# Falling decays by a backward scan, and the weight conversion in a written order

## The chip, the cores and the metric

The kernel runs on one core of one Trainium2 chip. The metric is device time in microseconds (us) of one execution; smaller is better. PE is the matrix engine (TensorE), DVE the vector engine, ACT the scalar engine, POOL GpSimd, SP the engine that issues most transfers. Every engine takes its instructions strictly in the order in which the program lists them, and engines wait for each other by semaphores.

## The reference

Shapes: q, k, v and f_logit are 4 batches x 8 heads x 768 tokens x 48; then x is 3072 tokens x 384, w_in 384 x 2048, w_out 2048 x 384. The two weights reach the kernel as 64-bit floats.

```python
f = 1.0 / (1.0 + np.exp(-f_logit))
for t in range(S):
    state = f[:, :, t, :, None] * state + np.einsum('bhd,bhe->bhde', k[:, :, t], v[:, :, t])
    y[:, :, t] = np.einsum('bhd,bhde->bhe', q[:, :, t], state)
...
h = x @ w_in                      # x: y with the heads next to each other
g = np.where(h > 0.0, h, np.exp(np.minimum(h, 0.0)) - 1.0)
return g @ w_out
```

## The kernel before

Tokens go in 12 units of U = 256 (three to a batch). Of each unit the kernel makes the attention, and then the MLP on PE: `up(P)` multiplies x with 256 columns of w_in, ACT makes Relu and Exp of it (`exped`), DVE joins them to the ELU (`elu`), and `down(P)` multiplies with 256 rows of w_out. P counts these pieces, eight to a unit. The units 0 and 1 use plain products; later ones use a scheme with fewer multiplications.

**Decays.** 1/f = 1 + exp(-f_logit) is made on ACT (`gates`). `grow` multiplies it up along the tokens with a scan on DVE; `fall` takes the reciprocal of all 256 values, which are the falling decays. k is multiplied with the first and q with the second (`scale`, on POOL). Heads go in pairs p = 0, 1, 2 of a layout of 64 rows each; the fourth pair (index NKT) is spread over the others' gaps: its decays are gathered by PE (`place`, psR), copied back by ACT, and its k and q are scaled then. `transposed`, `advance` (psU), `scores` (psS), `mask`, `step` (the states), `outputs` and `carried` (psY) finish the attention. Unit 0 goes through this first, with `first_outputs` in place of the last two; its x tile is what up(0) waits for.

**Weights.** The 64-bit words come in 16 parts of 768 KB, in the order in which they are needed: wi0, wi1, wi2, wo0, wi3, wo1, wi4, wo2, wi5, wo3, wi6, wo4, wi7, wo5, wo6, wo7 (parts 0 to 15; wi is a piece of w_in, wo of w_out). A part goes through `split` (two DVE operations, L628 and L632), `lower` (ACT, L638) and `merge` (DVE, L646), each of which needs the one before. `merge(n)` also issues `fetch(n + 7)`, since there are seven raw buffers; `split` has two buffers for its bits, so split(n) needs merge(n - 2).

**Order.** The program lists the work by hand. While units 0 and 1 go through the MLP, steps T = 0 to 31 alternate: an even T holds up(T/2), an odd T holds down(T//2 - 2). What stands at a step ahead of it comes from a table that `at_step` fills: attention of unit 1 at the steps in A1 (`both(1)` is advance, scores, mask and states), the fetch of unit 2 (`load(2)`) at step 8. Ahead of each even step stands the elu of the piece before. merge(n) stands two or three steps ahead of the step that needs the part, and split and lower two steps ahead of their merge, behind that step's own products. A transfer takes one of eight completion semaphores in turn, SP's and ACT's from one round, and its issue waits until the last transfer on that semaphore has landed.

Of the kernel before, what the change touches and what calls it, by code (L numbers as in the profile page):

```python
# [8 lines left out]
FP32 = mybir.dt.float32  # L9
# [4 lines left out]
ALU = mybir.AluOpType  # L14
# [342 lines left out]
def fast(ctx: ExitStack, tc: tile.TileContext, q, k, v, f_logit, w_in, w_out, out, flag, outer):  # L357
# [97 lines left out]
    NB = 2  # L455

    qkf = [
        {n: cst.tile([128, HP, 2, U] if n == "f" else [128, HP, U], FP32, name=f"{n}{i}") for n in "fqk"}
        for i in range(NB)
    ]  # L460
    src = {"q": q, "k": k, "f": f_logit}
# [4 lines left out]
    def load(u, names="fkqv"):  # L466
        b, s0 = u // UPB, (u % UPB) * U
        for n in names.replace("v", ""):
            to = qkf[u % NB][n][MAIN]
            frm = src[n][b, :, :, s0 : s0 + U].rearrange("(p r) d s -> (r d) p s", r=2)  # L470
            if n == "f":
                to, frm = to[:, 0:NKT, 0], frm[:, 0:NKT]
            nc.sync.dma_start(out=to, in_=frm)
            for r in range(2 if n == "f" or n == "k" and u > 1 else 0):
                gap = qkf[u % NB][n][GAP[r] : GAP[r] + PAD, 0:NKT]
                nc.sync.dma_start(
                    out=gap[:, :, 0] if n == "f" else gap,
                    in_=src[n][b, 2 * NKT + r, :, s0 : s0 + U].rearrange("(i j) s -> i j s", i=PAD),
                )
        if "v" in names:  # L480
            nc.sync.dma_start(
                out=vs[u % NB][:, :, PAD : PAD + DM], in_=v[b, s0 : s0 + U].rearrange("(c t) n -> t c n", t=W)
            )
# [186 lines left out]
    def gates(u, pieces=(NKT,), bias=1):  # L670

        p = 0
        for n in pieces:
            a = qkf[u % NB]["f"][:, p : p + n, 0]
            nc.scalar.activation(a, a, AF.Exp, scale=-1.0)
            if bias:
                nc.scalar.activation(a, a, AF.Copy, bias=1.0)
            p += n

    def scale(u, *todo):  # L680

        t = qkf[u % NB]
        for n, p, e in todo:
            e.tensor_tensor(out=t[n][:, p], in0=t[n][:, p], in1=t["f"][:, p, "kq".index(n)], op=ALU.mult)  # L684

    def grow(u, p):

        g = qkf[u % NB]["f"][:, p, 0]
        nc.vector.tensor_tensor_scan(out=g, data0=g, data1=g, initial=1.0, op0=ALU.mult, op1=ALU.max)  # L689

    def fall(u, p):

        f = qkf[u % NB]["f"]
        nc.vector.reciprocal(f[:, p, 1], f[:, p, 0])  # L694
# [9 lines left out]

    def place(u, which, bank, pairs=range(NKT)):

        f = qkf[u]["f"]
        if 0 in pairs:
            placed[u, which] = ps.tile([128, U], FP32, tag=bank, name=f"psR{u}_{which}")
        to = placed[u, which]  # L710
        for p in pairs:
            nc.tensor.matmul(to[:], lhsT=rows[:, p], rhs=f[:, p, which], start=p == 0, stop=p == NKT - 1)  # L712
        if NKT - 1 in pairs:
            nc.scalar.copy(f[:, NKT, which], to[:])  # L714

    def decays(u, p):
        grow(u, p)
        fall(u, p)
        scale(u, ("k", p, nc.gpsimd))
        if p:  # L720
            scale(u, ("q", p - 1, nc.gpsimd))
        if p == NKT - 1:
            move(u, slice(0, 2), nc.sync if u > 1 else nc.scalar)

    def watch(u):
        nc.vector.scalar_tensor_tensor(
            out=fine[:], in0=qkf[u % NB]["f"][:, 0:NKT, 0, U - 1 :], scalar=LIMIT, in1=fine[:],
            op0=ALU.is_le, op1=ALU.mult,
        )

# [26 lines left out]
    def step(u, c):  # L757

        if u % UPB == UPB - 1 and c == NC - 1:
            return  # L760
        new = pus[u][c % 2][:, c // 2]
        box = boxes[(u * NC + c) % len(boxes)]
        s = box[:].rearrange("n (p d) -> n p d", d=64)[:, 0:HP, PAD:]
        if u % UPB or c:
            old = sts[u, c][:].rearrange("n (p d) -> n p d", d=64)[:, 0:HP, PAD:]
            nc.vector.tensor_tensor(out=s, in0=new, in1=old, op=ALU.add)
        else:
            nc.scalar.copy(s, new)
        if c == NC - 1:
            end = qkf[u % NB]["f"][:, :, 1, U - 1 :].broadcast_to([128, HP, D])  # L770
            nc.vector.tensor_tensor(out=s, in0=s, in1=end, op=ALU.mult)
        sts[(u, c + 1) if c < NC - 1 else (u + 1, 0)] = box

# [89 lines left out]
    def first_outputs(part):  # L863
# [31 lines left out]
                            )  # L895
        if part == 0:
            for b in range(2):
                nc.scalar.copy(between[:, :, 0:NKT], first_y[b][:, :, :, 0])
# [7 lines left out]
    plan, later, hooks = {}, {}, []  # L906

    def at_step(step, *todo):
        plan.setdefault(step, []).extend(todo)

    def both(u):

        advance(u)
        mask(u, scores(u, ("m3", "m0")))
        while hooks:
            hooks.pop(0)()
        if u == 1:
# [296 lines left out]
    for c in range(NC - 1):
# [64 lines left out]
    def all_down(P):  # L1279
        for _ in down(P):  # L1280
            pass

    for T in range(PLAIN_UP * NFT):
        P = T // 2
        if T % 2 == 0 and P and P != NP:
            elu(P - 1)
        for f in plan.pop(T, ()):
            f()
        if T % 2 == 0:
            up(P)  # L1290
        elif P >= LAG:
            all_down(P - LAG)
        for n in later.pop(T, ()):
            split(n)
            if n not in (A1[2], A1[2] + 1, NFT - 1):
                lower(n)
# [30 lines left out]
    for s in range(5 * total // 2):  # L1327
# [84 lines left out]
```

## Time and profile before

| | us |
|---|---|
| median of 3 runs (545.68 to 546.71) | 545.69 |
| the profiled execution | 544.88 |
| its span | 542.5 |
| PE busy in it | 531.3 |
| DVE busy | 407.0 |
| ACT busy | 317.0 |
| POOL busy | 339.2 |

In the rows of the timeline the first number is the start in us from the span's start, the second the length of the group, then engine, line, operation, output and input with their sizes, the count, and in brackets the idle time of the engine just ahead of it and what ended it. A matmul of 32-bit floats shows as two records, so an `up` of six matmuls reads x12.

### The profile page before, as it was taken

To read this page: it belongs to the slowest core of one execution; us is meant where nothing else is said; L and a number is where in the kernel's file an instruction comes from. 1 tells how busy PE (TensorE), PEld (TensorE's weight loads), DVE (VectorE), ACT (ScalarE), POOL (GpSimd) and SP (SyncE) were. 2 spreads that over 40 slices of the span, in tenths; PEclk is the share of its full clock that TensorE was granted. 3 is DMA by queue.
4 is the path that set the end of the run, shared out by engine and by line. 5 is a ranking of instruction groups with operands and counts; after the bars stand their busy time and mean duration, and the time that the engine had idled before them with its cause. 6 is when DMAs were issued, how large, how long until landed. Compare 5 with 4: busy or idle time off the path is not lost.

```text
span 542.5 us, 15672 instructions
## 1 busy us (share of the span) xinstructions
PE 531.3 (98%) x6308; PEld 496.4 (91%) x6308; DVE 407.0 (75%) x717; ACT 317.0 (58%) x649; POOL 339.2 (63%) x560
## 2 busy tenths in 40 slices
PE   7999999999999999999999999999999999999996
PEld 3677778899999999999999999999999999999995
DVE  8898979866978887687787687687777876645563
ACT  4578774146564576566567467566665565574441
POOL 8320237688898398298298298388478467464452
PEclk9989999999999999999999999999999999999999
DMA  8999961023152271161271261262252212210001
GB/s 210 252 257 250 266 188 45 3 66 90 38 127 73 62 196 37 57 201 31 62 202 32 60 189 47 60 159 76 62 145 89 62 35 77 60 39 1 30 1 37
DMA packets 39347, 53.91 MB, mean 99 GB/s; under 512 B 4288, under 2 KB 29088, under 8 KB 39264
## 3 DMA queue, kind: packets, MB, share of 16 engines
q1 hardware_dynamic: 38848, 52.51, 36.4%
q8 instruction: 52, 0.85, 0.7%
q10 hardware_dynamic: 416, 0.30, 0.2%
q14 instruction: 31, 0.25, 0.2%
HBM read 45.02 MB, written 4.72 MB: 92 GB/s over the span
## 4 chain that ended last, share of the span: by engine, by line
PE 91%; DMA 5%; DVE 2%; SPq 0%; issue 0%; POOL 0%; ACT 0%; DVEq 0%; ACTq 0%; POOLq 0%
PE psM L1082 37%; PE psH L984 33%; PE psH L1008 7%; PE psM L1044 4%; DMA area<-in_moe_w_in_dram 4%; PE psY L823 2%; PE psY L847 2%; PE psU_a L808 2%; PE psS L785 2%; PE psT L745 1%; DMA f<-in_f_logit_dram 1%; DVE vals L974 1%; DVE gg L1018 0%; PE psR L712 0%; DVE at L793 0%
## 5 line engine op out<-in xcount | busy, mean ns | idle before, releaser
L1031 POOL TENSOR_TENSOR sums<-gg 128x128 f32<-128x128 f32 x172 | 101.7, 610 | 123.1 <-DVE gg L1018 121.1
L990 ACT COPY vals<-psH 128x512 f32<-128x512 f32 (+1 forms) x120 | 65.4, 545 | 123.3 <-PE psH L984 123.1
L984 PE MATMUL psH<-xt,wi 128*128 128x128 f32 x880 | 131.4, 276 | 0.1
L974 DVE TENSOR_TENSOR vals<-vals,psH 128x256 f32<-128x256 f32 (+1 forms) x160 | 61.7, 386 | 84.4 <-PE psH L984 43.2
L984 PE MATMUL psH<-xt,area 128*128 128x128 f32 x720 | 118.2, 278 | 0.1
L984 PEld LDWEIGHTS psH<-xt,wi 128*128 128x128 f32 x880 | 115.2, 192 | 0.7 <-DVE gg L1018 0.3
L1082 PE MATMUL psM<-area,sums 128*128 128x192 f32 x516 | 103.4, 327 | 0.0
L984 PEld LDWEIGHTS psH<-xt,area 128*128 128x128 f32 x720 | 100.9, 192 | 1.8 <-ACT psH L992 0.3
L1082 PEld LDWEIGHTS psM<-area,sums 128*128 128x128 f32 x516 | 85.9, 191 | 0.0
L1082 PE MATMUL psM<-wo,gg 128*128 128x192 f32 x376 | 76.6, 329 | 0.0
L1018 DVE SCALAR_TENSOR_TENSOR gg<-gg,vals 128x512 f32<-128x512 f32 x80 | 64.0, 835 | 9.7 <-ACT gg L999 7.9
L974 DVE TENSOR_TENSOR vals<-vals 128x256 f32<-128x256 f32 x120 | 64.3, 550 | 2.0
L694 DVE RECIPROCAL f<-f 128x256 f32<-128x256 f32 x36 | 62.8, 1748 | 1.0
L1082 PEld LDWEIGHTS psM<-wo,gg 128*128 128x128 f32 x376 | 61.1, 191 | 1.6 <-DVE at L793 1.4
L999 ACT ACTIVATE gg<-gg 128x512 f32<-128x512 f32 x96 | 60.5, 630 | 3.1
L684 POOL TENSOR_TENSOR k<-k,f 128x256 f32<-128x256 f32 x48 | 37.7, 787 | 36.4 <-DVE f L689 15.0
L998 ACT ACTIVATE gg<-vals 128x512 f32<-128x512 f32 x80 | 49.5, 619 | 17.1 <-DVE vals L974 15.0
L964 POOL TENSOR_TENSOR xt<-xt 128x256 f32<-128x256 f32 x57 | 48.6, 866 | 3.1 <-DVE xt L964 1.7
L684 POOL TENSOR_TENSOR q<-q,f 128x256 f32<-128x256 f32 x48 | 40.4, 843 | 14.4 <-ACT f L714 9.8
L1008 PE MATMUL psH<-xt,wi 128*128 128x256 f32 x192 | 46.2, 392 | 1.2 <-DVE wi L646 1.1
L1031 POOL TENSOR_TENSOR sums<-sums,gg 128x128 f32<-128x128 f32 x86 | 47.3, 549 | 0.2
L1031 POOL TENSOR_TENSOR sums<-gg,sums 128x128 f32<-128x128 f32 x86 | 40.9, 475 | 6.6
(115 smaller groups left out, 747.5 us busy)
## 6 DMA issues: line engine op xcount, KB each, us to landing
area<-in_moe_w_out_dram SPq DMA_DIRECT2D x16, 384.0 KB, 7.8
again<-in_moe_w_in_dram SPq DMA_DIRECT2D x16, 384.0 KB, 4.3
again<-in_moe_w_out_dram SPq DMA_DIRECT2D x16, 384.0 KB, 3.5
k<-in_k_dram SPq DMA_DIRECT2D x12, 384.0 KB, 4.0
q<-in_q_dram SPq DMA_DIRECT2D x12, 384.0 KB, 5.3
v<-in_v_dram SPq DMA_DIRECT2D x12, 384.0 KB, 5.9
area<-in_moe_w_in_dram SPq DMA_DIRECT2D x24, 192.0 KB, 6.9
out_dram<-o SPq DMA_DIRECT2D x42, 96.0 KB, 1.7
```

The lines of the kernel that those rows point to most:

```text
L684: e.tensor_tensor(out=t[n][:, p], in0=t[n][:, p], in1=t["f"][:, p, "kq".index(n)], op=ALU.mult)
L694: nc.vector.reciprocal(f[:, p, 1], f[:, p, 0])
L964: e.tensor_tensor(out=pick(x, to), in0=pick(x, a), in1=pick(x, b), op=ALU.subtract)
L974: nc.vector.tensor_tensor(out=pick(v, to), in0=x, in1=y, op=op)
L984: nc.tensor.matmul(bank[:, slot], lhsT=w_block(q, w), rhs=xts[m][:, x], start=(i < 2 and t == 0), stop=True, skip_group_check=True,)
L990: nc.scalar.copy(v[:, at : at + size], bank[:, frm : frm + size])
L998: nc.scalar.activation(g[:], h, AF.Relu, scale=-1.0)
L999: nc.scalar.activation(g[:], g[:], AF.Exp, scale=-1.0)
L1008: nc.tensor.matmul(ph[:, i], lhsT=wi[j][:, kt, i * 128 : (i + 1) * 128], rhs=xts[m][:, 2 * kt : 2 * kt + 2].rearrange("n t f -> n (t f)"), ...
L1018: nc.vector.scalar_tensor_tensor(out=g[:], in0=g[:], scalar=-1.0, in1=phs.pop(P), op0=ALU.add, op1=ALU.max)
L1031: nc.gpsimd.tensor_tensor(out=s[:, i], in0=x, in1=y, op=op)
L1082: nc.tensor.matmul(pm[bank][:, half * DH : (half + 1) * DH], lhsT=x, rhs=y, start=first, stop=(j == NP - 1), skip_group_check=True,)
```

## The change

It has three parts.

1. `fall` takes the reciprocal of the last column alone and runs the scan backward over the gates from there, with a negative step. To keep the gates, the tile of f is one row of 528 columns per pair: grown decays in columns 0 to 255, gates in 256 to 511, and the falling decays over them, shifted by one column. `move` copies 513 columns instead of 512.
2. Of unit 0, k and q are scaled on DVE, right behind their scans; POOL keeps the fourth pair's k. q of the fourth pair is multiplied from psR directly. The two small copies `between` go from ACT to DVE, all masks come ahead of states 1 to 3, and gates(1) moves behind the scores.
3. splits, merges, elus and unit 1's falls stand in two tables, ahead of a step's products (`BEFORE`) and behind them (`BEHIND`). `F1` goes from 6 to 5 and `both(1)` from step 9 to step 7.

```diff
-    F1 = 6
+    F1 = 5
...
-    A1 = (4, 9, 11, 12)
+    A1 = (4, 7, 11, 12)
...
     def fall(u, p):
         f = qkf[u % NB]["f"]
-        nc.vector.reciprocal(f[:, p, 1], f[:, p, 0])
+        nc.vector.reciprocal(f[:, p, 2 * U : 2 * U + 1], f[:, p, U - 1 : U])
+        back = f[:, p, 2 * U : U : -1]
+        nc.vector.tensor_tensor_scan(out=back, data0=back, data1=back, initial=1.0, op0=ALU.mult, op1=ALU.min)
...
     for p in range(NKT):
         grow(0, p)
-        scale(0, ("k", p, nc.gpsimd))
...
+        scale(0, ("k", p, nc.vector))
+        place(0, 0, "m2", (p,))
...
+    for p in range(NKT):
+        fall(0, p)
+        scale(0, ("q", p, nc.vector))
...
-    for n in range(1, NFT):
-        t = min(max(needs[n][0] - 2, 0), n) + 2 * (n == NFT - 1)
-        if t != A1[1]:
-            at_step(t, lambda n=n: merge(n))
-        if n > 1:
-            later.setdefault(max(min(t, n) - 2, 0), []).append(n)
...
+    EVENTS = {"m": merge, "s": word, "e": elu, "f": fallen}
+    BEFORE = {
+        0: "m1", 2: "e0 m2", 4: "e1", 5: "m3", 6: "e2 m4", 7: "s6 m5", 8: "e3", 9: "m7", 10: "e4 m8", 11: "m9",
+        12: "e5 m10", 13: "m11", 14: "e6 m12", 15: "e7", 16: "m14", 17: "m15",
+    }
+    BEHIND = {
+        0: "f0 s2", 1: "f1", 2: "f2 s3", 5: "s4", 6: "s5", 7: "s7", 8: "s8", 9: "s9", 10: "s10", 11: "s11", 12: "s12",
+        13: "s13", 14: "m13 s14", 15: "s15",
+    }
```

(`word(n)` is split(n) and lower(n); both(1) now calls merge(6).)

**ACT, from up(2) to up(4) of unit 0.** `gg0_2` is the ELU tile of piece 2, L638 (`area`) is lower, kn and f1 are unit 1's. Before:

```order
L638 ACTIVATE area_139<-area_139 128x768 x2
L749 COPY kn_76<-psT1_0_484 128x512
L749 COPY kn_76<-psT1_1_490 128x512
L998 ACTIVATE gg0_2_520<-psH0_2_513 128x512
L999 ACTIVATE gg0_2_520<-gg0_2_520 128x512
L638 ACTIVATE area_139<-area_139 128x768 x2
L714 COPY f1_71<-psR1_1_549 128x256
L998 ACTIVATE gg0_3_561<-psH0_3_554 128x512
L999 ACTIVATE gg0_3_561<-gg0_3_561 128x512
```

And with the change:

```order
L638 ACTIVATE area_139<-area_139 128x768
L754 COPY kn_76<-psT1_0_475 128x512
L754 COPY kn_76<-psT1_1_481 128x512
L1003 ACTIVATE gg0_2_511<-psH0_2_504 128x512
L1004 ACTIVATE gg0_2_511<-gg0_2_511 128x512
L719 COPY f1_71<-psR1_1_520 128x256
L638 ACTIVATE area_139<-area_139 128x768
L1003 ACTIVATE gg0_3_547<-psH0_3_540 128x512
L1004 ACTIVATE gg0_3_547<-gg0_3_547 128x512
L638 ACTIVATE area_139<-area_139 128x768 x3
```

Counted from the start of the program, the rows of lower before are parts 4 and 5 ahead of piece 2's Relu and Exp and 6 and 7 behind them; with the change, part 3 stands ahead of piece 2, part 4 behind it, and parts 5, 6 and 7 behind piece 3.

**DVE, around unit 1's mask and states.** The output wi or wo with `bits5` is merge(5), bits with area is split. Before:

```order
L646 ISA wi_137<-area_139,bits8_564 128x1536
L628 TENSOR_SCALAR bits10_602<-area_139 128x768
L632 TENSOR_SCALAR area_139<-area_139 128x768
L793 TENSOR_TENSOR at1_640<-psS1_0_641,twice_109 128x512
L793 TENSOR_TENSOR at1_640<-psS1_1_642,twice_109 128x512
L646 ISA wo_138<-area_139,bits9_576 128x1536
```

And with the change:

```order
L646 ISA wo_138<-area_139,bits5_550 128x1536
L798 TENSOR_TENSOR at1_598<-psS1_0_599,twice_109 128x512
L798 TENSOR_TENSOR at1_598<-psS1_1_600,twice_109 128x512
L646 ISA wi_137<-area_139,bits6_554 128x1536
L771 TENSOR_TENSOR state4_120<-psU1_a0_564,state3_119 128x4x48
...
L776 TENSOR_TENSOR state2_118<-state2_118,f1_71 128x4x48
L628 TENSOR_SCALAR bits7_647<-area_139 128x768
```

Mask and states stood behind split(10) and around merge(9); they stand ahead of split(7) now, with merge(6) between them.

**SP, at the end of the weights.** f, k, q and v into the tiles of unit 0 are load(2). Before:

```order
L608 DMA area<-in_moe_w_out_dram 128x384 x6
L473 DMA f_68<-in_f_logit_dram 96x3x256
L476 DMA f_68<-in_f_logit_dram 16x3x256 x2
L473 DMA k_70<-in_k_dram 96x4x256
L476 DMA k_70<-in_k_dram 16x3x256 x2
L473 DMA q_69<-in_q_dram 96x4x256
L481 DMA v_74<-in_v_dram 128x2x384
```

And with the change:

```order
L608 DMA area<-in_moe_w_out_dram 128x384 x2
L473 DMA f_68<-in_f_logit_dram 96x3x256
L476 DMA f_68<-in_f_logit_dram 16x3x256 x2
L473 DMA k_70<-in_k_dram 96x4x256
L476 DMA k_70<-in_k_dram 16x3x256 x2
L473 DMA q_69<-in_q_dram 96x4x256
L481 DMA v_74<-in_v_dram 128x2x384
L608 DMA area<-in_moe_w_out_dram 128x384 x4
```

Parts 14 and 15 (wo6 and wo7, four transfers) stood ahead of load(2) and stand behind it now. In the round of eight semaphores, the last small k transfer of load(2) shares one with the first of ACT's two transfers of unit 1's x (L864, issued by `carried(1)` at step 12), and the v transfer with the second; before, that was so for the v transfer and one transfer of load(3).

More of the change, by code (lines that the diff above doesn't have):

```diff
@@ L457, in fast @@
     qkf = [
-        {n: cst.tile([128, HP, 2, U] if n == "f" else [128, HP, U], FP32, name=f"{n}{i}") for n in "fqk"}
+        {n: cst.tile([128, HP, 2 * U + PAD] if n == "f" else [128, HP, U], FP32, name=f"{n}{i}") for n in "fqk"}
         for i in range(NB)
@@ L476, in load @@
                 nc.sync.dma_start(
[L477 removed]
+                    out=gap[:, :, 0:U] if n == "f" else gap,
                     in_=src[n][b, 2 * NKT + r, :, s0 : s0 + U].rearrange("(i j) s -> i j s", i=PAD),
@@ L668, in check, with gates @@
         nc.scalar.activation(hi, hi, AF.Exp, scale=-(2.0**26), accum_out=spans[:, 0, n : n + 1])
-    def gates(u, pieces=(NKT,), bias=1):
+    GROWN, GATES, FALLEN = slice(0, U), slice(U, 2 * U), slice(U + 1, 2 * U + 1)
+    def gates(u, pieces=(NKT,)):
         p = 0
         for n in pieces:
[L674 to L677, printed above, removed]
+            f = qkf[u % NB]["f"][:, p : p + n]
+            nc.scalar.activation(f[:, :, GROWN], f[:, :, GROWN], AF.Exp, scale=-1.0)
+            nc.scalar.activation(f[:, :, GATES], f[:, :, GROWN], AF.Copy, bias=1.0)
             p += n
@@ L705, in place @@
     def place(u, which, bank, pairs=range(NKT)):
-        f = qkf[u]["f"]
+        f, which_ = qkf[u]["f"], (GROWN, FALLEN)[which]
         if 0 in pairs:
@@ L711, in place @@
         for p in pairs:
-            nc.tensor.matmul(to[:], lhsT=rows[:, p], rhs=f[:, p, which], start=p == 0, stop=p == NKT - 1)
+            nc.tensor.matmul(to[:], lhsT=rows[:, p], rhs=f[:, p, which_], start=p == 0, stop=p == NKT - 1)
         if NKT - 1 in pairs:
-            nc.scalar.copy(f[:, NKT, which], to[:])
+            nc.scalar.copy(f[:, NKT, which_], to[:])
     def decays(u, p):
@@ L722, in decays @@
         if p == NKT - 1:
-            move(u, slice(0, 2), nc.sync if u > 1 else nc.scalar)
+            move(u, slice(0, 2 * U + 1), nc.sync if u > 1 else nc.scalar)
     def watch(u):
         nc.vector.scalar_tensor_tensor(
-            out=fine[:], in0=qkf[u % NB]["f"][:, 0:NKT, 0, U - 1 :], scalar=LIMIT, in1=fine[:],
+            out=fine[:], in0=qkf[u % NB]["f"][:, 0:NKT, U - 1 : U], scalar=LIMIT, in1=fine[:],
             op0=ALU.is_le, op1=ALU.mult,
@@ L897, in first_outputs @@
             for b in range(2):
-                nc.scalar.copy(between[:, :, 0:NKT], first_y[b][:, :, :, 0])
+                nc.vector.tensor_copy(between[:, :, 0:NKT], first_y[b][:, :, :, 0])
             return
@@ L904, in first_outputs @@
             copy(to[FULL[r], 1], first_y[1][FULL[1 - r]])
-    plan, later, hooks = {}, {}, []
+    plan, hooks = {}, []
     def at_step(step, *todo):
@@ L917, in both @@
         if u == 1:
-            merge(A1[1])
+            merge(6)
         for c in range(NC):
@@ L1201, in fast @@
     )
+    for p in range(NKT):
+        fall(0, p)
+        scale(0, ("q", p, nc.vector))
+    place(0, 1, "m2", (0,))
+    transposed(0, 1, "m1", (1,))
     pc = scores(0, ("m3", "m0"), (0,))
+    advance(0)
+    step(0, 0)
+    place(0, 1, "m2", (1,))
     scores(0, None, (1,), pc)
-    fall(0, 2)
-    scale(0, ("q", 2, nc.gpsimd))
     place(0, 1, "m2", (2,))
+    nc.vector.tensor_tensor(out=qkf[0]["q"][:, NKT], in0=qkf[0]["q"][:, NKT], in1=placed[0, 1][:], op=ALU.mult)
     scores(0, None, (2,), pc)
-    for c in range(1, NC - 1):
-        step(0, c)
-    scale(0, ("q", NKT, nc.gpsimd))
     scores(0, None, (NKT,), pc)
     warm(1, "m1")
+    gates(1)
     mask(0, pc)
+    for c in range(1, NC):
+        step(0, c)
     for c in range(NC - 1):
@@ L1224, in fast @@
     lower(0)
+    split(1)
     for p in range(NKT - 1):
@@ L1234, in fast @@
     at_step(1, lambda: place(1, 0, "m3"), lambda: scale(1, ("k", NKT, nc.gpsimd)))
-    for p in range(NKT):
-        at_step(p + 1, lambda p=p: fall(1, p), lambda p=p: scale(1, ("q", p, nc.gpsimd)))
     at_step(F1 - 1, lambda: watch(0), lambda: watch(1))
-    at_step(A1[2], lambda: outputs(1, ("m3", "m0")), lambda: lower(A1[2]), lambda: lower(A1[2] + 1))
-    for n in range(1, NFT):
-        t = min(max(needs[n][0] - 2, 0), n) + 2 * (n == NFT - 1)
-        if t != A1[1]:
-            at_step(t, lambda n=n: merge(n))
-        if n > 1:
-            later.setdefault(max(min(t, n) - 2, 0), []).append(n)
+    at_step(A1[2], lambda: outputs(1, ("m3", "m0")))
     at_step(F1, lambda: place(1, 1, "m0"))
@@ L1251, in fast @@
     at_step(8, lambda: load(2))
-    at_step(15, lambda: elu(NP - 1), lambda: gates(2), lambda: lower(NFT - 1))
+    at_step(15, lambda: gates(2))
     attention(2, D2, A2)
@@ L1281, in all_down, with word, fallen, events @@
             pass
+    def word(n):
+        split(n)
+        lower(n)
+    def fallen(p):
+        fall(1, p)
+        scale(1, ("q", p, nc.gpsimd))
+    EVENTS = {"m": merge, "s": word, "e": elu, "f": fallen}
[7 more added lines that the diff above has]
+    }
+    def events(todo):
+        for e in todo.split():
+            EVENTS[e[0]](int(e[1:]))
     for T in range(PLAIN_UP * NFT):
         P = T // 2
-        if T % 2 == 0 and P and P != NP:
+        if T % 2 == 0 and P > NP:
             elu(P - 1)
+        events(BEFORE.get(T, ""))
         for f in plan.pop(T, ()):
@@ L1292, in fast @@
             all_down(P - LAG)
[L1293 to L1296, printed above, removed]
+        events(BEHIND.get(T, ""))
     def products():
@@ L1356, in fast @@
         take((4, 4, 3, 3)[s] if s < 4 else (CHUNKS if T < base(NU - 1) else ENDING)[s % 10])
-    assert not plan and not later
+    assert not plan
     exp_quad(total - 1, 5 * total // 2)
```

29 lines of the change are left out of this document (7 added, 22 removed).

## The prediction

> **What bounds the kernel now.** I read three views in this order: the page's busy shares and slices, busy time by stretches, and the chain of waits. The page's busy time of each engine, its share of the span and the instructions:
>
> ```profile
> PE 531.3 (98%) x6308; PEld 496.4 (91%) x6308; DVE 407.0 (75%) x717; ACT 317.0 (58%) x649; POOL 339.2 (63%) x560
> ```
>
> PE is nearly full. Busy time by stretch (PE, PEld, DVE, ACT, POOL, then granted clock, DMA share, GB/s):
>
> ```profile
> 50.00:60.00 10.00, 10.00 (x171) 7.19 (x162) 9.51 (x18) 6.94 (x9) 2.15 (x3) 1.00 1.02 290
> 70.00:80.00 10.00, 10.00 (x41) 7.41 (x40) 7.67 (x9) 7.58 (x10) 3.74 (x5) 1.00 0.76 206
> 130.00:542.00 412.00, 406.93 (x4970) 397.90 (x4969) 298.21 (x560) 243.45 (x547) 270.35 (x447) 1.00 0.28 78
> ```
>
> While the weights are converted (to about 85 us) PE never waits in these stretches, though DVE is 95% busy between 50 and 60. Behind 130 us PE works 406.93 of 412. So what PE loses early is lost at the end too. The chain of waits over the conversion (start, length):
>
> ```profile
> 31.91 0.91 DVE wi L646
> 32.96 4.39 PE psH L1008 x12
> 37.35 2.70 PE psM L1044 x8
> 40.06 1.29 PE psR L712 x6
> 41.35 2.59 PE psH L1008 x12
> 43.94 2.58 PE psM L1044 x8
> 49.11 1.08 PE psU_a L808 x64
> 50.19 0.95 PE psS L785 x64
> 56.51 1.09 PE psY L823 x64
> 60.37 1.09 PE psY L847 x64
> 74.59 2.58 PE psM L1044 x8
> ```
>
> These are up(2), down(0), place, up(3), down(1); then unit 1's psU, psS, outputs and carried; the last is down(6). From 32.96 on PE follows upon PE. One wait is left, before up(2), and one weak stretch behind it (PE's timeline; then a quarter of a microsecond with its busy time, clock, DMA share and GB/s):
>
> ```profile
> 23.35 2.86 PE L1008 MATMUL psH<-xt,wi 128*128 128x256 f32 x12
> 30.90 0.94 PE L1155 MATMUL psW<-ident 128*1 128x1 f32 x32
> 32.96 4.39 PE L1008 MATMUL psH<-xt,wi 128*128 128x256 f32 x12 [1.12 <-DVE wi L646]
> 34.25:34.50 0.25, 0.25 (x2) 0.50 1.01 221
> ```
>
> A 1.12 us wait behind 0.94 us of one-column matmuls was followed by half clock: up(2) took 4.39 for the usual 2.59, so 2 × 1.8 = 3.6 us at half speed.
>
> **The change part by part**, as delay of PE against the profiled execution.
>
> *A, the front: up(0), at 23.35 before.* Unit 0's work on DVE and POOL, and unit 1's conversion costs, in timeline, tile and group rows:
>
> ```profile
> 5.63 0.69 DVE L689 TENSOR_TENSOR_SCAN f<-f 128x256 f32<-128x256 f32 x1 [0.60 <-ACT f L677]
> 8.49 4.94 DVE L694 RECIPROCAL f<-f 128x256 f32<-128x256 f32 x3
> 6.89 3.64 POOL L684 TENSOR_TENSOR k<-k,f 128x256 f32<-128x256 f32 x4 [0.22 <-DMA k<-in_k_dram]
> L974 DVE TENSOR_TENSOR vals<-vals 128x256 f32<-128x256 f32 x120 | 64.3, 550 | 2.0
> 41.04 0.37 DVE L726 SCALAR_TENSOR_TENSOR fine<-f,fine 128x3 f32<-128x3 f32 x2
> L689 DVE TENSOR_TENSOR_SCAN f<-f x36: 666/814/1211, 5.6 to 441.2; 128x256 f32<-128x256 f32 x36
> 16.05 1.29 DVE L793 TENSOR_TENSOR at<-psS,twice 128x512 f32<-128x512 f32 x2 [2.02 <-PE psS L785]
> 17.71 0.36 DVE L771 TENSOR_TENSOR state<-state,f 128x192 f32<-128x192 f32 x1
> 19.12 0.36 ACT L898 COPY between<-psY 128x6 f32<-128x6 f32 x2 [4.51 <-PE psY L892]
> ```
>
> k arrives at 6.89, so three products (0.55) and two more scans (0.69) end at 9.9. Then each pair takes a one-column reciprocal, a backward scan and a product. The reciprocal of one column has no row; I take 0.12, between nothing and the 0.18 of L726. The backward scan has none either; I take the forward 0.69, from 0.67 up to L689's slowest 1.21, or, if a negative step is as slow as the reciprocal, 1.65. That is 1.36 a pair: the third scan ends at 9.9 + 2 × 1.36 + 0.81 = 13.4, against 8.49 + 4.94 = 13.43. **The reciprocals' time is spent on products that POOL did beside them.** Place, its copy, the product of the fourth q and its scores follow as before, but that product takes 0.55 on DVE for some 0.9 on POOL (3.64 / 4), so the mask comes some 0.4 earlier than 16.05. Behind the mask, two more state operations (0.7) and the two copies (0.36) now stand on DVE ahead of the conversion of wi0: up(0) moves **+0.6** (+0.2 at the lower bounds; +2.2 with scans of 1.21, +3.5 with 1.65).
>
> *B, before up(2).* Falls of 0.8 in place of 1.65 (4.94 / 3) on DVE, three of them ahead of it or beside it, bring wi2 to about 31.0, ahead of PE at 32.4. The wait (1.12) and the half clock (4.39 − 2.59) go: **−2.9** (0 if another stall takes their place).
>
> *C to G, the written order.* Its pieces in the trace, Relu, Exp, lower, psR's copy (ACT), merge, states and split (DVE):
>
> ```profile
> 56.54 0.60 ACT L998 ACTIVATE gg<-psH 128x512 f32<-128x512 f32 x1 [0.68 <-PE psH L1008]
> 57.17 0.63 ACT L999 ACTIVATE gg<-gg 128x512 f32<-128x512 f32 x1
> 53.95 1.92 ACT L638 ACTIVATE area<-area 128x768 uint16<-128x768 uint32 x1
> 46.22 0.47 ACT L714 COPY f<-psR 128x256 f32<-128x256 f32 x1
> 54.75 0.95 DVE L646 CUSTOM_DVE_ANT_0 wo<-area,bits 128x1536 uint16<-128x1536 uint16 x1
> 55.62 1.74 DVE L766 TENSOR_TENSOR state<-psU_a,state 128x192 f32<-128x192 f32 x4
> 57.39 0.83 DVE L771 TENSOR_TENSOR state<-state,f 128x192 f32<-128x192 f32 x1
> 58.14 0.55 DVE L628 TENSOR_SCALAR bits<-area 128x768 int32<-128x768 int32 x1
> 58.72 0.56 DVE L632 TENSOR_SCALAR area<-area 128x768 int32<-128x768 int32 x1
> ```
>
> lower(n) now stands on ACT behind the Relu and Exp of the piece just multiplied, and merge(n) directly ahead of the product that needs it. From the end of an up: 0.2 to hand over, 1.25 for Relu and Exp, 1.92 lower, 0.95 merge, **4.3 us**. Where PE has less than that between, it waits:
> - C, up(3) (wi3): up(2) ends at 35.0; place is ahead of down(0) now, its copy ends at 37.0, lower 39.0, merge 40.0; PE is there at 35.0 + 1.29 + 2.58 = 38.9. **+1.2** (0.8 to 1.6).
> - D, down(1) (wo1): both(1) has been moved between, 1.08 + 0.95 of PE. 4.3 − 2.0 = **+2.3** (1.9 to 2.6).
> - E, down(2) (wo2): DVE from the end of merge(5): mask 1.29, merge(6) 0.95, states 1.74 + 0.83, split(7) 1.12, then lower(7) 1.92 and merge(7) 0.95, 8.8, less some 0.2 by which such rows overlap. PE has down(1) and up(4), 2.58 + 2.59. **+3.4** (2.9 to 3.8).
> - F, up(5) (wi5): lower(7) ends 0.95 before down(2) starts; Relu and Exp 1.25, lower(8) 1.92, merge(8) 0.95 end 3.2 behind its start, against its 2.58. **+0.6** (0 to 0.9).
> - up(6) has outputs, down(3) and carried between, 1.09 + 2.58 + 1.09 = 4.8: nothing. down(3), down(4) and down(5) have parts whose lower stands one piece ahead: nothing.
> - G, up(7) (wi7): only down(4) between. 4.3 − 2.6 is 1.7; an ELU on DVE stands ahead of the merge too and can take up to 0.5 more: **+1.9** (1.5 to 2.2).
>
> The sum so far is 0.6 − 2.9 + 1.2 + 2.3 + 3.4 + 0.6 + 1.9 = +7.1; PE is ready for down(6) at 81.7.
>
> *H, down(6) (wo6 and wo7).* SP issues load(2) ahead of the last four transfers now, and its last small k transfer waits for ACT's first x transfer. Such a wait is in the trace (SP's waits: total, times, longest), with the copies ahead of the x transfer and its size and landing:
>
> ```profile
> SPq L481 <- DMA xt<-xt: 3.6, 1, 3.6
> 66.83 1.18 ACT L856 COPY xt<-psY 64x512 f32<-64x512 f32 x2
> xt<-xt ACTq DMA_DIRECT2D x2, 48.0 KB, 2.8
> ```
>
> Before, only v stood behind it. carried(1) ended at 61.46 and ends at 66.7 now (+5.2 by then); with the copies and 2.8 the transfer lands at about 71.3. Then SP issues 48 KB, q, v and four transfers of 384 KB, 2.35 MB, at 206 to 290 GB/s (the stretches above): 9.4 us at 250, and some 2 to the landing, so wo7 is there at 82.7. split(15) stands ahead of merge(14): 1.12 + 0.95, 84.8. **+3.1** (0 at 290 without a delay; 5.9 at 206 with 2.8).
>
> *Clock.* Behind one of these stalls I take one half-clock stretch like the traced one, **+1.8** (0 to 5.4, three). The Trainium skill, "TensorE: Matmul & The Clock Gate", section "HAM oscillation — how this bites in real kernels", gives the rule that PE should have no idle gap over about 3.4 us. The trace disagrees, with half clock behind 1.12 us idle and 0.94 us of thin work; by the rule only E touches the limit, which is the one stretch taken here, and by the row each stall pays, which is a rival below.
>
> *Costed at nothing.* 30 of the 36 falls come later, under PE's 406.93 of 412; DVE has 298.21 busy there, so their cheapening buys nothing, and would cost nothing if it were reversed. move's one column more goes the same way.
>
> **Sum:** 7.1 + 3.1 + 1.8 = +12.0; 544.88 + 12.0 = 556.9. The median is 0.81 above the profiled execution: **557.7 us**.
>
> **The rivals.**
> 1. *The transfers are hidden anyway*: H is 0, because wo6's raw words come early enough or the rate is that of 50 to 60. For it speaks that 290 was reached; against, that the wait on x is fixed by ACT. 557.7 − 3.1 = 554.6 (552.8 without a clock stretch).
> 2. *Half clock behind every long stall*, C, E and H: 557.7 + 2 × 1.8 = 561.3. For it speaks the up(2) row; against, that no thin matmuls stand ahead of these.
> 3. *The other side: the conversions keep up*, and just A and B count, −2.3: 543.4. It is decided at up(3) and down(1): lower must end within PE's work between. If lower(5) ran ahead of piece 3's Relu and Exp, 4.3 would be 3.1, and one buffer's slack would carry to E; the order on ACT, where it stands behind them, speaks against. For it speaks that DVE, 95% busy at 50 to 60, gets some 2.5 us of falls off its hands (3 × 0.85).
> 4. *No net change*: the stalls come to just the 2.3 that A and B save, 545.7.
>
> **How the numbers follow.** Forecast 0.56, rival 1 0.16, rival 2 0.18, rival 3 0.06, rival 4 0.03, and 0.01 for slower by less. A measurement of this kernel can tell 0.2%, 1.1 us, from no change. Slower: 0.56 + 0.16 + 0.18 + 0.01 = 0.91; same 0.03; faster 0.06. The likeliest case's own range is 554.5 to 561; with rival 1 down to 551.5 and rival 2, with the upper bound of H, up to 564 it holds 8 in 10.
>
> **What would show it.** Right: up(0) near 24.0; no wait before up(2); PE waits ended by merge (wi or wo, L646) before up(3), down(1), down(2), up(7) and down(6), of the sizes above; a Relu and Exp directly ahead of lower on ACT; SP waiting for an x transfer while DMA idles between 64 and 72; clock 0.5 for some 3.6 us behind a stall. Wrong: up(0) at 25 or later (slow backward scans); no wait at down(1), which would leave only B; wo7 landing before 80; waits by anything but merge; or a change of PE's time behind 130 us.

## The result, and the profile after

The changed kernel takes 560.15 us (median of 4 runs, 558.32 to 560.49), the kernel before 545.68 (4 runs, 544.73 to 546.71): 1.0258 times as long, 95% interval 1.0229 to 1.0287. Forecast were 557.7 and a range of 551.5 to 564. Sign and size came out; two of the terms behind them did not.

The profiled execution took 558.32 us, its span 556.6 for 542.5. The page's busy times and PE's timeline in the changed kernel (start, length, operation, and in brackets PE's idle time just ahead and what ended it):

```profile
PE 533.2 (96%) x6308; PEld 495.9 (89%) x6308; DVE 386.7 (69%) x762; ACT 316.9 (57%) x647; POOL 343.4 (62%) x553
...
24.32 2.86 PE L1013 MATMUL psH<-xt,wi 128*128 128x256 f32 x12 [0.65 <-DVE xt L909]
33.20 2.86 PE L1013 MATMUL psH<-xt,wi 128*128 128x256 f32 x12
41.44 2.83 PE L1013 MATMUL psH<-xt,wi 128*128 128x256 f32 x12 [1.39 <-DVE wi L646]
48.42 4.54 PE L1049 MATMUL psM<-wo,gg 128*128 128x384 f32 x8 [2.12 <-DVE wo L646]
56.57 2.85 PE L1049 MATMUL psM<-wo,gg 128*128 128x384 f32 x8 [1.02 <-DVE wo L646]
59.88 2.83 PE L1013 MATMUL psH<-xt,wi 128*128 128x256 f32 x12 [0.46 <-DVE wi L646]
74.69 2.83 PE L1013 MATMUL psH<-xt,wi 128*128 128x256 f32 x12 [1.66 <-DVE wi L646]
83.88 2.85 PE L1049 MATMUL psM<-wo,gg 128*128 128x384 f32 x8 [1.19 <-DVE wo L646]
129.92 0.71 PE L989 MATMUL psH<-xt,wi 128*128 128x128 f32 x4 [1.29 <-DVE gg L1023]
```

DVE is busy 20 us less, PE 2 us more, and the span is 14 us longer: a saving off the path. The rows are up(0), up(2), up(3), down(1), down(2), up(5), up(7) and down(6). The wait before up(2) is gone and up(2) takes 2.86 for 4.39. Six new waits, each ended by a merge (L646), stand where the prediction put steps C to H. The ninth row, near 130 us, was not foreseen.

How far each place of PE's work has moved, from the starts of unit 2's, unit 3's and the last unit's psU, and the end of PE's last product:

| | before | changed | moved |
|---|---|---|---|
| unit 2's psU | 96.32 | 105.88 | +9.6 |
| unit 3's psU | 132.91 | 143.61 | +10.7 |
| the last psU | 468.24 | 481.28 | +13.0 |
| PE's last product ends | 537.32 | 550.07 | +12.8 |
| the span ends | 542.5 | 556.6 | +14.1 |

So 9.6 us are lost in the conversion, and 4.5 behind it, where the prediction had nothing.

### The profile page after: what moved, and what is told of

The parts are those of the page before. It is cut to its first block, busy times and chain, and to the rows that moved or that the text cites. A ratio compares the mean times of both kernels' runs of the same rounds, so it can differ in the third digit from the quotient of the medians.

```text
span 556.6 us, 15713 instructions
## 1 busy us (share of the span) xinstructions
PE 533.2 (96%) x6308; PEld 495.9 (89%) x6308; DVE 386.7 (69%) x762; ACT 316.9 (57%) x647; POOL 343.4 (62%) x553
## 4 chain that ended last, share of the span: by engine, by line
PE 61%; POOL 19%; DMA 10%; DVE 5%; ACT 2%; issue 2%; SPq 1%; POOLq 0%; DVEq 0%; ACTq 0%
PE psM L1087 25%; PE psH L989 24%; POOL sums L1036 11%; DMA area<-in_moe_w_in_dram 5%; POOL xt L969 5%; PE psH L1013 4%; DMA area<-in_moe_w_out_dram 3%; PE psY L828 2%; DVE vals L979 2%; PE psU_a L813 2%; PE psS L790 1%; ACT area L638 1%; POOL k L685 1%; PE psT L750 1%; DMA f<-in_f_logit_dram 1%
## 5 line engine op out<-in xcount | busy, mean ns | idle before, releaser
L1036 POOL TENSOR_TENSOR sums<-gg 128x128 f32<-128x128 f32 x172 | 99.6, 598 | 118.1 <-DVE gg L1023 117.3
L989 PE MATMUL psH<-xt,wi 128*128 128x128 f32 x880 | 133.0, 276 | 3.0 <-POOL xt L969 1.7
L989 PEld LDWEIGHTS psH<-xt,wi 128*128 128x128 f32 x880 | 115.8, 192 | 4.8 <-POOL xt L969 3.1
L685 POOL TENSOR_TENSOR k<-k,f 128x256 f32<-128x256 f32 x45 | 42.7, 950 | 38.7 <-DMA k<-in_k_dram 17.0
L979 DVE TENSOR_TENSOR vals<-vals 128x256 f32<-128x256 f32 x120 | 63.1, 540 | 2.0
L1036 POOL TENSOR_TENSOR sums<-sums,gg 128x128 f32<-128x128 f32 x86 | 49.7, 578 | 0.2
L1036 POOL TENSOR_TENSOR sums<-gg,sums 128x128 f32<-128x128 f32 x86 | 45.2, 525 | 6.6
L1013 PE MATMUL psH<-xt,wi 128*128 128x256 f32 x192 | 44.9, 383 | 4.2 <-DVE wi L646 3.5
L1013 PEld LDWEIGHTS psH<-xt,wi 128*128 128x128 f32 x192 | 35.7, 190 | 12.4 <-issue 5.5
L969 POOL TENSOR_TENSOR xt<-xt 128x256 f32<-128x256 f32 x57 | 42.2, 754 | 4.4 <-DVE xt L969 3.0
L1087 PE MATMUL psM<-wo,sums 128*128 128x192 f32 x172 | 42.8, 331 | 0.0
```

Source lines behind the costliest of these rows:

```text
L969: e.tensor_tensor(out=pick(x, to), in0=pick(x, a), in1=pick(x, b), op=ALU.subtract)
L979: nc.vector.tensor_tensor(out=pick(v, to), in0=x, in1=y, op=op)
L989: nc.tensor.matmul(bank[:, slot], lhsT=w_block(q, w), rhs=xts[m][:, x], start=(i < 2 and t == 0), stop=True, skip_group_check=True,)
L1013: nc.tensor.matmul(ph[:, i], lhsT=wi[j][:, kt, i * 128 : (i + 1) * 128], rhs=xts[m][:, 2 * kt : 2 * kt + 2].rearrange("n t f -> n (t f)"), ...
L1036: nc.gpsimd.tensor_tensor(out=s[:, i], in0=x, in1=y, op=op)
L1087: nc.tensor.matmul(pm[bank][:, half * DH : (half + 1) * DH], lhsT=x, rhs=y, start=first, stop=(j == NP - 1), skip_group_check=True,)
```

## The experiments

The two theories were set against each other first. Theory 1: the written order costs what is lost by 96 us, and the backward scans from unit 2 on slow POOL and cost the rest. The rival: the late loss follows from the late weights, and the scans cost nothing.

**Backward scans alone** (the decay's layout and `fall` as changed; all else as before):

> The kernel before with the first part of the change alone: all falls by a one-column reciprocal and a backward scan; unit 0's scaling and the order of the weights as before. Theory 1 (a backward scan with its two operands slows POOL beside it, which costs PE from unit 2 on): the wait before up(2) and its half clock go (-2.9 by the prediction's step B), and 2 to 4 us come back behind 125 us, so 544.5 to 547, with PE waits ended by POOL's xt products. Rival (the loss behind 125 us comes from the late weights, the later scans cost nothing): 542.5 to 543.5, and no PE wait ended by POOL.

545.79 us (10 runs), 1.0004 times before, 0.9981 to 1.0026. PE's waits behind 95 us in this kernel:

```profile
PE psH L989 <- POOL xt L969: 1.8, 7, 0.6
```

Up to 133 us it stands 0.25 ahead of the kernel before; by the last psU it is 1.7 behind. Theory 1's time and its waits, without any written order. The early gain was smaller than expected, since PE waited 0.78, 0.24 and 0.91 us before up(2), down(0) and up(4).

**Scans and the front**:

> The first two parts of the change, the order of the weights as before. Theory 1: up(0) is about 1 us late as in the changed kernel (24.3), up(2) gains what is left of step B, the late loss of 2 to 4 us is there: 545.5 to 548. Rival: 543 to 545. Either way no PE waits before up(3), down(1), down(2), up(7) and down(6), if these come from the written order.

546.54 us (10 runs), 1.0009 times, 0.9994 to 1.0024. up(0) starts at 24.74 for 23.35, and yet unit 2's psU is 0.2 ahead of before: what the front loses, the cheaper falls give back. No wait of the written order is in it: PE waits for merges 0.2 us at most. Behind that it loses as the kernel with scans alone does.

**The written order alone**, with reciprocals and POOL's scaling:

> The third part alone: the written order of the weights, with reciprocals and unit 0's scaling as before. Both theories: PE waits before up(3), down(1), down(2), up(5), up(7), down(6) as in the changed kernel, and the wait with half clock before up(2) stays, so unit 1's pieces are 9 to 12 us late at 90 us. Theory 1: nothing more behind 125 us, total 555 to 557.5. Rival: 2 to 4.5 more behind 125 us, 558 to 561.

557.35 us (4 runs), 1.021 times, 1.0178 to 1.0243. Its PE timeline:

```profile
41.52 2.83 PE L1008 MATMUL psH<-xt,wi 128*128 128x256 f32 x12 [1.39 <-DVE wi L646]
48.50 4.54 PE L1044 MATMUL psM<-wo,gg 128*128 128x384 f32 x8 [2.13 <-DVE wo L646]
56.65 2.85 PE L1044 MATMUL psM<-wo,gg 128*128 128x384 f32 x8 [1.02 <-DVE wo L646]
74.71 2.83 PE L1008 MATMUL psH<-xt,wi 128*128 128x256 f32 x12 [1.66 <-DVE wi L646]
83.96 2.85 PE L1044 MATMUL psM<-wo,gg 128*128 128x384 f32 x8 [1.25 <-DVE wo L646]
```

These are the changed kernel's waits to within 0.1 us, and unit 2's psU is 9.6 late here too. **The whole early loss belongs to the written order**; scans and front neither add to it nor take from it, since the next conversion resets PE's time. (PE's wait before up(2) was replaced by one of 0.90 on POOL's k, without half clock; that was not expected.) Behind 133 us it loses 0.9.

**Reciprocals again from unit 2 on**, in the changed kernel:

```diff
     def fall(u, p):
         f = qkf[u % NB]["f"]
+        if u > 1:
+            nc.vector.reciprocal(f[:, p, FALLEN], f[:, p, GROWN])
+            return
```

> The changed kernel, but the falls of units 2 to 11 by the reciprocal of all 256 values; units 0 and 1 and the order are as changed. Theory 1: the shift of 9.5 at 96 us stays and the loss behind 125 us goes, 556 to 557.5; POOL's k products take about 735 ns in the mean there again, for 941. Rival: the loss stays, 559.5 to 560.5.

557.39 us, 1.0199 times, 1.0174 to 1.0223: 2.8 less than the changed kernel's median, theory 1's range. Its psU does not move further between unit 3 and the last (+12.2 and +12.2), and no PE wait is ended by POOL. Its profiled execution alone would not show the gain: it ends just 0.9 earlier than the changed kernel's, since unit 2's psU is 10.6 late in it and the wait near 130 us (below) is there too. POOL's k products between 130 us and the end in the kernel before and in the changed one, and between 140 and 480 us in this one (busy, mean ns, idle before):

```profile
L684 POOL TENSOR_TENSOR k<-k,f 128x256 f32<-128x256 f32 x32 | 23.5, 735 | 8.7 <-DVE f L689 7.7 <-DMA f<-f 1.0
```

```profile
L685 POOL TENSOR_TENSOR k<-k,f 128x256 f32<-128x256 f32 x33 | 31.0, 941 | 7.9 <-DVE f L691 7.9
```

```profile
L685 POOL TENSOR_TENSOR k<-k,f 128x256 f32<-128x256 f32 x32 | 23.7, 740 | 8.8 <-DVE f L691 7.6 <-DMA f<-f 1.2
```

735, 941, 740 ns: with the scan POOL's product becomes slower, and without it quick again. In one unit, DVE and POOL side by side, before:

```profile
210.97 1.75 DVE L694 RECIPROCAL f<-f 128x256 f32<-128x256 f32 x1
212.64 1.87 DVE L1018 SCALAR_TENSOR_TENSOR gg<-gg,vals 128x512 f32<-128x512 f32 x2
...
211.68 0.45 POOL L1031 TENSOR_TENSOR sums<-gg,sums 128x128 f32<-128x128 f32 x1
212.09 0.72 POOL L684 TENSOR_TENSOR k<-k,f 128x256 f32<-128x256 f32 x1
212.78 1.18 POOL L684 TENSOR_TENSOR q<-q,f 128x256 f32<-128x256 f32 x1
```

and in the changed kernel:

```profile
222.53 0.98 DVE L699 TENSOR_TENSOR_SCAN f<-f 128x256 f32<-128x256 f32 x1
223.43 2.01 DVE L1023 SCALAR_TENSOR_TENSOR gg<-gg,vals 128x512 f32<-128x512 f32 x2
...
223.04 0.72 POOL L1036 TENSOR_TENSOR sums<-gg,sums 128x128 f32<-128x128 f32 x1
223.72 1.17 POOL L685 TENSOR_TENSOR k<-k,f 128x256 f32<-128x256 f32 x1
224.86 1.08 POOL L685 TENSOR_TENSOR q<-q,f 128x256 f32<-128x256 f32 x1
```

Beside the reciprocal, which reads one tensor, POOL's sums take 0.45 and its k product 0.72. Beside the scan, which reads two, the sums take 0.72; then DVE comes to its two-operand ELU 0.8 us earlier against POOL's list, and k, which used to fall into the reciprocal's time, now falls into the ELU's and takes 1.17. **The slow reciprocal had been POOL's undisturbed time.** The scan too is slower beside POOL: 0.98 for the 0.69 that it took in unit 0.

How this reaches PE shows in unit 3 of the kernel with scans alone, which up to there keeps step with the kernel before to within 0.3 us. POOL's product of x that the next up waits for starts at 160.97 for 160.31, though POOL's five products of x ahead of it even took less (3.71 for 4.15), and PE waits 0.63 us for it.

The Trainium skill, "GPSIMD Engine Reference", section "1. Specifications", says that POOL's interfaces to SBUF are shared with VectorE, with contention where a DVE instruction has two SBUF inputs. The rows agree in kind (0.45 to 0.72, 0.72 to 1.17). The prediction should have weighed this rule: it speaks against the change.

**Unit 2's load later** in the changed kernel:

```diff
-    at_step(8, lambda: load(2))
+    at_step(11, lambda: load(2))
```

> The changed kernel with unit 2's load three steps later (step 11 for 8), so that SP issues the last four weight transfers ahead of it, as in the kernel before. If the load's place on SP's queue is what makes wo6 and wo7 late (step H), SP's long wait for the x transfer stands behind them, wo7 lands before 70, and down(6) waits for nothing: 1.2 us of PE's waiting goes, 558.5 to 559.5. If the transfers' own rate or DVE's backlog sets down(6), the wait stays: 559.8 to 560.8.

555.49 us (4 runs), 1.0163 times, 1.0127 to 1.0199. The wait before down(6) is gone, as step H has it; SP still waits 11.4 us for the x transfer, now with nothing urgent behind it. The time fell by 4.7, though, not by 1.2. In the profiled execution only 0.5 less is lost by 96 us, since a half-clock stretch came behind down(2) (4.37 us for 2.85), where no wait before a later conversion made up for it. The wait near 130 us was absent (below), so that unit 3's psU is 8.7 late for 10.7. The rest of the 4.7 is not accounted for by this trace, which ends 2.8 earlier than the changed kernel's first and 1.2 earlier than its second (below).

**Lower ahead of Relu and Exp** in the changed kernel:

```diff
-        0: "m1", 2: "e0 m2", 4: "e1", 5: "m3", 6: "e2 m4", 7: "s6 m5", 8: "e3", 9: "m7", 10: "e4 m8", 11: "m9",
-        12: "e5 m10", ...
+        0: "m1", 2: "e0 m2", 4: "e1 s4", 5: "m3", 6: "e2 m4 s5", 7: "s6 m5 s7", 8: "e3 s8", 9: "m7", 10: "e4 m8 s10", 11: "m9",
+        12: "e5 m10 s12", ...
...
-        0: "f0 s2", 1: "f1", 2: "f2 s3", 5: "s4", 6: "s5", 7: "s7", 8: "s8", 9: "s9", 10: "s10", 11: "s11", 12: "s12",
+        0: "f0 s2", 1: "f1", 2: "f2 s3", 9: "s9", 11: "s11",
```

(An s is split and lower together, so the splits move with them.)

> The changed kernel with split and lower of parts 4, 5, 7, 8, 10 and 12 ahead of the step's products in the table, so that ACT does them ahead of that piece's Relu and Exp; merges, the load and all else as changed. If lower's place behind Relu and Exp makes the waits, those before up(3), down(1), up(5) and up(7) shrink by about the 1.25 us of these two, the one before down(2) with them: 4 to 6 us less, 554 to 556.5. If the raw words' landing or DVE's backlog makes them, they stay: 559 to 561.

553.32 us (4 runs), 1.0135 times, 1.0097 to 1.0172; 6.8 less than the changed kernel, more than the 4 to 6 expected, and unit 2's psU is 5.9 late for 9.6. The gain did not come where it was expected, though. The waits before down(1) and down(6) went and there was no half clock, and 1.56 were left before down(2). But those before up(3), up(5) and up(7) stayed at 1.83, 1.03 and 1.57. Ahead of up(3) on DVE:

```profile
40.25 0.69 DVE L1023 SCALAR_TENSOR_TENSOR gg<-gg,psH 128x512 f32<-128x512 f32 x1 [2.82 <-ACT gg L1004]
40.85 1.16 DVE L646 CUSTOM_DVE_ANT_0 wi<-area,bits 128x1536 uint16<-128x1536 uint16 x1
```

lower had ended at 38.2, but merge(4) stands behind the ELU of piece 2, and that waits for piece 2's Exp, now later on ACT. The order has two rows on two engines that do the same: behind Exp on ACT, behind the ELU on DVE.

**Load, lower and late reciprocals together**:

> Lower ahead of Relu and Exp, the load at step 11, and the reciprocal of all 256 values from unit 2 on, together on the changed kernel. If the three causes are separate, their gains add: 560.2 less 5, 1.2 and 2.8, 550 to 552.5. If one hides behind another (fewer waits only bring the next one out), 553 to 557.

553.55 us, 1.0137 times, 1.0099 to 1.0175: no better than lower ahead alone, the second theory's figure. Its profiled execution had a front 1.3 us later and the wait near 130 us again.

**Lower ahead and late reciprocals**, without the later load:

> Lower ahead of Relu and Exp, and the reciprocal of all 256 values from unit 2 on, with unit 2's load at step 8 as changed. If POOL's slowing by the late scans costs about 1.5 us whatever the early part does, 551 to 552.5; if the late reciprocals bring nothing once the early waits are shorter, 553 to 554.

551.73 us (4 runs), 1.0109 times, 1.0068 to 1.0149: 1.6 less than with scans, by the medians of two sets of runs whose ranges overlap.

**Four merges ahead of the ELUs**, on top of it:

```diff
-        ... 6: "e2 m4 s5", ... 10: "e4 m8 s10", ... 12: "e5 m10 s12", ... 14: "e6 m12",
+        ... 6: "m4 e2 s5", ... 10: "m8 e4 s10", ... 12: "m10 e5 s12", ... 14: "m12 e6",
```

> As the kernel with lower ahead of Relu and Exp and late reciprocals, and merges 4, 8, 10 and 12 stand ahead of the ELU of the piece before on DVE. In its trace lower was done early, yet the waits before up(3), up(5) and up(7) were still 1.9, 1.0 and 1.6, with the merge directly behind that ELU. If the ELU's place is what is left, these three go: 551.7 less 4.5, 546.5 to 548.5. If something else holds the merges (DVE's splits, or the raw words), less than half goes: 549.5 to 552.

550.49 us (5 runs), 1.0097 times, 1.0066 to 1.0127. The three waits are gone, so the ELU's place was what held them, though the time lies in the other theory's range. It fell by 1.2 for 4.5, because other waits came out: 0.31, 0.49 and 0.44 before down(1), up(4) and down(5), and above all this one before down(6):

```profile
80.44 2.85 PE L1052 MATMUL psM<-wo,gg 128*128 128x384 f32 x8 [2.17 <-DVE wo L646]
```

PE now comes to down(6) earlier and waits for the parts that SP issues behind unit 2's load; SP's wait for the x transfer lies between these four transfers here.

**And the load at step 11**:

> The last kernel (lower first, four merges ahead of the ELUs, late reciprocals) with unit 2's load at step 11 for 8. In the last one the waits before up(3), up(5) and up(7) went, but down(6) waited 2.2 us again, PE having come there earlier than wo6 and wo7. If the load's place on SP's queue sets their landing (step H), the two waits of 0.4 and 2.2 before down(5) and down(6) go: 547.5 to 549. If not, 550 to 551.

550.62 us (6 runs), 1.0081 times, 1.0054 to 1.0109: the expectation fell. The wait before down(6) went, and unit 2's psU is 2.9 late for 6.1; by unit 3's it is 4.6, by the last 5.1 (5.5 in the kernel without). 1.5 of what was gained went into the waits near 125 to 133 us; the rest comes back piece by piece. Of the written order's waits 0.31, 0.49 and 1.66 us are left, before down(1), up(4) and down(2). No run took both(1) back to step 9, so whether its place holds the last one is not shown.

**The wait near 130 us.** Five of the fourteen profiled executions have it, and just these five have x transfers of unit 2 that took 2.8 us or more in the median of the two; the others have 2.2. The changed kernel once more:

> The changed kernel once more, unaltered, for a second profiled execution. In the first, and in the kernels with late reciprocals under the written order, PE waited 1.2 to 1.5 us near 128 us for an ELU, behind a transfer of unit 2's x that took 2.9 to 3.0 us for 2.2 elsewhere. If that is chance of one execution, the second may show 2.2 and no such wait, and its span is then 1 to 1.5 shorter by it; if the changed program brings it about, 2.9 and the wait are there again.

556.75 and 560.2 us. It was there again: 0.98 us of waiting, the transfer at 2.8. The transfer in the changed kernel's first execution and in the one before the change (engine, kind, count, KB each, us to landing):

```profile
xt<-xt SPq DMA_DIRECT2D x2, 48.0 KB, 2.9
```

```profile
xt<-xt SPq DMA_DIRECT2D x2, 48.0 KB, 2.2
```

Behind it DVE's blend of x comes late, behind that the ELU, and PE waits for that. It is in the changed kernel twice, with late reciprocals, in the one with load, lower and reciprocals and in the last one; it is not in the written order alone, nor with the load later alone, nor with lower ahead. No single part of the change brings it.

The DMA packets of the traces show what the transfer meets. Each of the two x transfers has 128 packets. Near the second one a single 16 KB packet of the queue `q8 instruction` passes, by its name program code (us from the issue of the second x transfer):

| | instruction packet | the transfer's last four packets start | landed |
|---|---|---|---|
| changed, first execution | 1.60 to 2.47 | 2.46 to 2.78 | 3.65 |
| changed, second execution | 1.19 to 2.23 | 2.23 to 2.47 | 3.33 |
| late reciprocals | 1.20 to 2.72 | 2.70 to 3.03 | 3.89 |
| load, lower, reciprocals | 1.29 to 2.50 | 2.48 to 2.81 | 3.67 |
| the last kernel | 1.27 to 2.33 | 2.33 to 2.50 | 3.35 |
| the nine others | starts at 1.58 to 2.16 | all started by 1.66 | 2.16 to 2.24 |

In the five, the last four packets start just when the instruction packet ends; in the nine, the transfer is through or nearly so when it comes. At about 1.6 it hit one execution of six, at 1.3 and earlier all four. So some tenths of a microsecond between two unrelated transfers decide on this wait. What sets the moment of the instruction packet, and with it which kernels are hit, no run shows.

The same second execution shows the clock. Its rows for down(1) and down(2):

```profile
48.65 2.85 PE L1049 MATMUL psM<-wo,gg 128*128 128x384 f32 x8 [2.12 <-DVE wo L646]
...
56.78 2.85 PE L1049 MATMUL psM<-wo,gg 128*128 128x384 f32 x8 [2.69 <-DVE wo L646]
```

The same program, the same 2.12 us of waiting before down(1), and full clock: 2.85 for 4.54. And down(2) starts as late as in the other execution, having waited 2.69 for 1.02.

The clock records of the traces show why. In each execution the granted clock changes only at whole multiples of 3.41 us behind the first record (8.06 + 12 × 3.41 = 49.0 in the first execution, whose records begin at 8.06), and each half-clock stretch inside the work is 3.41 us long. The interval ahead of the half clock in the first execution and the half-clock one, then the two intervals that the wait before down(1) touches in the second, whose records begin at 7.42 (stretch, its length, busy time of PE, PEld, DVE, ACT and POOL, granted clock, DMA share, GB/s):

```profile
45.61:49.02 3.41, 1.29 (x50) 1.02 (x43) 1.61 (x3) 3.41 (x2) 0.00 (x0) 1.00 1.08 230
49.02:52.44 3.42, 3.42 (x6) 1.68 (x6) 3.07 (x8) 0.07 (x1) 0.00 (x0) 0.50 1.05 277
...
44.97:48.38 3.41, 1.56 (x108) 1.42 (x100) 0.74 (x1) 3.38 (x4) 0.00 (x0) 1.00 1.08 227
48.38:51.79 3.41, 3.14 (x11) 2.03 (x12) 3.20 (x7) 0.94 (x1) 0.00 (x0) 1.00 1.05 284
```

The whole wait of 2.12 us lies in one interval of the first execution (3.41 less 1.29). The second cuts it into 1.85 and 0.27, and the one of 2.69 before down(2) into 1.12 and 1.57. In all fourteen executions, from 22 us on, an interval in which PE was idle for 2.12 us or more was followed by half clock, and none with 1.91 us or less, but for the one in the kernel before: there 1.12 us of idling and the one-column matmuls come to 1.99. So the place of a wait in this grid decides as well as its length.

**Scans for units 0 and 1 alone**, in the kernel before:

> The kernel before with backward scans for units 0 and 1 alone; units 2 to 11 take the reciprocal of all 256 values. Theory 1 (the late scans cost 1.5 to 2.5 by slowing POOL, the early ones relieve DVE ahead of up(2)): no PE wait ended by POOL's xt products behind 140 us, 543.5 to 545, faster than before by 1 to 2. Rival (the early gain is not there either): 545.5 to 546.5.

545.49 us (12 runs) for 546.16, 0.9979 times, 0.9959 to 0.9999. Its median is the lowest of all, 0.5 above theory 1's range and at the lower edge of the rival's: that it beats the kernel before is just at the edge of what these runs can tell. POOL's xt products end no PE wait in it, but it still loses 1.1 between unit 3 and the last.

**All traces together.** From unit 3's psU to the last, the six executions with late scans take 1.4 to 2.3 us more than the kernel before; the seven others with reciprocals take -0.4 to 1.2 more. The groups don't overlap; their means differ by 1.3 us. Up to the psU of the last unit but one they lie further apart, 1.6 to 2.2 against -0.4 to 0.5. And in each of the six, PE waits for POOL's xt products six or seven times, 1.5 to 1.8 us in all; in none of the other eight does it wait for them behind 95 us.

## Why the prediction was right, and where it was not

- **Sign and mechanism: right.** The waits stand before up(3), down(1), down(2), up(5), up(7) and down(6), each ended by a merge, and the written order alone makes them.
- **A, the front: right in its parts.** The one-column reciprocal takes 0.16 (assumed 0.12), the backward scan 0.69 (0.69), a product 0.42 (0.55). up(0) came 1.0 late for 0.6, and in other executions of the same front 1.0 to 2.5. What was missed is that this matters little: the next conversion resets PE's time.
- **B: right in kind.** The wait and the half clock went; up(2) ends about 1.3 earlier than before, for 2.3 by A and B together.
- **C to G**: waits of 1.39, 2.12, 1.02 (2.69 in the second execution), 0.46 and 1.66 for 1.2, 2.3, 3.4, 0.6 and 1.9. E was over-sized: the last state operation took 0.36, not the 0.83 of the row that was used. "Behind Relu and Exp" was only half the cause in C, F and G. The merge's place behind the ELU on DVE, named for G as "0.5 more", holds these three by itself.
- **H: right, too large.** SP waited 11.3 us for the x transfer, the DMA share between 64 and 72 us was 0.05, and the chain of waits runs from it through SP's issues to down(6):

```profile
68.99 2.23 DMA xt<-xt
...
74.54 7.17 DMA area<-in_moe_w_out_dram
81.76 0.04 issue
81.81 0.57 DVE bits L628
82.40 0.56 DVE area L632
82.96 0.88 DVE wo L646
```

  wo7 landed at 81.7 for 82.7. PE was late by more than assumed at that place, and waited 1.19 for 3.1.
- **Clock: the term was wrong, not the event.** One half-clock stretch came in the first execution, of 4.54 us for 2.85. But it cost about nothing there: it lies inside the time until merge(7), which sets down(2) anyway (E's wait shrinks by 1.67). The +1.8 should not have been added to E. Where it came behind down(2) instead, with the late reciprocals (4.54) and with the later load (4.37), it did cost: up(6) starts 44.2 us behind up(0) there, for 43.0 in the changed kernel's second execution. The prediction counted waits by their length alone; the grid of 3.41 us was missed. The Trainium skill's rule of no idle gap over about 3.4 us ("TensorE: Matmul & The Clock Gate", "HAM oscillation — how this bites in real kernels") is not borne out as a limit: 2.12 us of idling was enough once.
- **"Costed at nothing": the step that failed.** "30 of the 36 falls come later ... so their cheapening buys nothing, and would cost nothing if it were reversed." The prediction named a change of PE's time behind 130 us and waits by anything but merge as signs against it, and both came. From unit 3's psU to the last, PE loses 2.3 us in this execution. In the mean over all traces, the late scans cost some 1.3 there by POOL's slowing, shown by taking them out and by putting in nothing but scans. Another 1.1 went between unit 2's psU and unit 3's, with the wait near 130 us. And 1.3 lie behind the last product: ten executions with the written order end 6.0 to 7.1 us behind it, the four others 5.1 to 5.6. In the changed kernel PE's own closing semaphore comes at 6.13 us behind it, when the other engines have passed theirs by 4.4; in the kernel before all pass by 4.6. What holds PE there stays open.

So the total was met since two errors partly cancelled, which is luck: 12.0 forecast and 9.6 measured by 96 us, 0 forecast and 4.5 behind it.

## What to carry to other kernels

In an order written by hand, what stands ahead of a conversion on its in-order engine counts more than what the conversion costs: put it ahead of the steps that wait for PE (Exp on ACT, the ELU on DVE), and look at each engine it passes. Before adding a transfer to a queue, look at which urgent ones it passes, and at what its issue may wait for. A slow operation with one operand beside a busy POOL may be cheaper than a quick one with two.

## What the runs showed of the hardware that was not expected

- A scan with a negative step costs the same 0.69 us as a forward one (128 x 256, floats); over the changed kernel, most of it beside POOL, it takes 0.98 in the median and 1.19 at most.
- A DVE operation with two operands can slow POOL's 128 x 256 product from 0.72 to 1.17 us; a reciprocal of the same size beside it does not.
- Half clock is not fixed by the program: the same wait of 2.12 us was followed by half clock in one execution and not in the other. In these traces the clock changes on a grid of 3.41 us that begins elsewhere in each execution, and what counts is PE's idle time within one interval (2.12 us or more, against 1.91 or less; 1.99 with one-column matmuls in it was enough too).
- A 16 KB packet of program code can hold the last four packets of a 48 KB transfer: it landed after 3.3 to 3.9 us for 2.2.
